# Reordering the attention stage of a retention + Mish + GLU kernel: weights decoded one round ahead, state copies first on ScalarE, v loaded before q and k

## The chip, the cores and the metric

The kernel runs on one core of a Trainium2 chip. The metric is the device time of one execution in microseconds. The engines are TensorE (PE in the profile, with its weight loads as PEld), VectorE (DVE), ScalarE (ACT), GpSimd (POOL) and SyncE (SP), which here issues nearly all transfers. Each engine works through its own queue in the order of issue.

## The reference

Three stages follow one another; the output of each is the input of the next. All data are float32.

```python
# 1: retention (linear attention with decay), B=2, H=8, S=768, D=64
for t in range(S):
    state = gamma * state + einsum('bhd,bhe->bhde', k[:, :, t], v[:, :, t])
    y[:, :, t] = D**-0.5 * einsum('bhd,bhde->bhe', q[:, :, t], state)
x = y.transpose(0, 2, 1, 3).reshape(1536, 512)
# 2: MLP, w_in 512 x 2048, w_out 2048 x 512
h = x @ w_in
x = (h * tanh(softplus(h))) @ w_out            # Mish
# 3: gated MLP, w_gate and w_val 512 x 1536, w_out 1536 x 512
out = (sigmoid(x @ w_gate) * (x @ w_val)) @ w_out
```

## The kernel before

The 1536 tokens are three chunks of 512 (`NCH`), or twelve blocks of 128 (`NSUB`); four blocks make a chunk (`SPC`), six blocks a batch entry (`SPB`).

**Two halves.** The first half, the attention stage, is issued exactly in the order of the code (`early` holds an element). After `early.clear()` the rest of the two MLPs is first recorded as nodes, and `replay()` issues them in an order that it plans from costs of its own; nothing in that second half is touched, and its plan starts from the same set of recorded nodes. At the seam, each engine goes on with the second half as soon as its queue has finished the first.

**Attention.** The products are small: a "quarter product" (`quarter`) is a 64x64 by 64x64 matmul that uses a quarter of the array. Block j needs `scores(j, r)` (k against q, masked by `mask` on VectorE into `a_t`), `state(j, s)` (k against the scaled v, `vp_t`, summed into one PSUM bank `st`), `keep` (ScalarE copies the running state out of that bank into `s_t`), and `outs(j, row)` (the block's own part and the part from the state). `at_prep(j)` is the GpSimd instruction that scales v into `vp`, and for j from 1 to 5 a second one that prepares a table `og`. `block(j)` issues, in this order: state and scores of block j+1 (first half) between the second row of outs of block j-1; the VectorE product that puts block j-1 into `acc_t`; `keep(j+1, 0)`; the first row of outs of block j between scores and state of block j+1 (second half); `mask`; `keep(j+1, 1)`. The second half's state products add to the bank that `keep(j+1, 0)` copies, so they wait for that copy, and the next block's state products wait for `keep(j+1, 1)`.

**Dense work inside the attention stage.** From block 4 on, one step of the first MLP is issued in each round. There are eight: `plain1(0)`, `plain1(1)` for the first chunk and `plain1(0, 1)`, `plain1(1, 1)` for the second, two steps each. A step is twelve 128x128 by 128x512 matmuls (`plain_steps`): values are split into a high and a low part, and each of four 128-row parts takes three products (high-high, high-low, low-high). Then ScalarE applies Mish (`e`), and `split` makes the high part on ScalarE and the low part on GpSimd (`g`). The split input of the first chunk is `xc` (`put_plain`), that of the second is `B11` and `B21` (`put_block`). The second chunk uses the weights of the first again.

**Weights.** They come as 512 KB pieces of 8-byte words (`load_piece`, two staging buffers `raw`) and are decoded by `decode`: two ScalarE instructions (`raw`, `v`), then two VectorE ones. `put` leaves the split (ScalarE `late_hi`, then VectorE or GpSimd `late_lo`) for later; `flush` issues what was left, `flush_hi` only the ScalarE part. `pump` flushes and then decodes one piece; `weight(key)`, which the dense step calls, flushes again.

**The round before** (`blocks`): `pump` (decode of the piece that this very round's dense step needs, in rounds 4 to 7), `block(j)` with `flush_hi()` in its middle, `at_prep(j+2)`, the loads, `load_piece`, in rounds 4 and 8 the split of the chunk's input, then the dense step, whose Mish and split stand last in ScalarE's queue. In rounds 8 to 11 the decoded piece belongs to `w_out` and no dense step of the stage needs it.

**Transfers.** k and v come together (`nv`, 3 buffers), q and k feature-major as `qk` (5 buffers), 512 KB each. Before, `load(jq, jn)` issues qk of block j+4 and then nv of block j+3, after block j.

Of the kernel before, what the change touches and what calls it, by code (L numbers as in the profile page):

```python
# [9 lines left out]
F32 = mybir.dt.float32  # L10
# [8 lines left out]
P = 128  # L19
# [4 lines left out]
def kernel(ctx, tc, qk, nv, w1i, w1o, w2g, w2v, w2o, ma_in, og_in, sg_in, ck_in, out):  # L24
# [12 lines left out]
    NSUB = qk.shape[0]  # L37
    KK = DM // P
    NP = KK
    D = P // 2  # L40
    FF1 = w1i.shape[0]
    FF2 = w2g.shape[0]
    N = 512
    NCH = NT // N
    SPC = N // P
    SPB = NSUB // 2
# [4 lines left out]
    AHEAD = 4  # L51
    Q = P // 2

    early = [True]
# [108 lines left out]
    dve = Queue(nc.vector, lambda n, kw: (0.157 + 0.00104 * n) * (1 if psum(kw) else 1.3), 0.1)  # L163
    act = Queue(nc.scalar, lambda n, kw: 0.17 + 0.0009 * min(n, N), 0.1)
    pool = Queue(nc.gpsimd, lambda n, kw: 0.08 + 0.00258 * n, 0.1)
    sync = Queue(nc.sync, lambda n, kw: 3.3 if isinstance(kw["out"], Part) else 1.6, 0.3)
# [98 lines left out]
    xc_t = big.tile([P, KK, 2, N], F32R, name="xc")  # L265
    acc_t = [big.tile([P, KK, N], F32, name=f"acc{c}") for c in range(NCH)]
    y_t = {"B11": xc_t[:, :2, :, :H], "B21": xc_t[:, 2:, :, :H], "T4": xc_t[:, :2, :, H:], "B22": xc_t[:, 2:, :, H:]}

    def split(raw, hi, lo, eng):
        act.activation(out=hi, in_=raw, func=AF.Copy)  # L270
        eng.tensor_tensor(out=lo, in0=raw, in1=hi.bitcast(F32), op=ALU.subtract)
# [33 lines left out]
    for f in range(FF2):  # L305
# [3 lines left out]
        a, q, w, o = [[(k, (2, f))] for k in "aqs"] + [[("o", (2, f - 1)), ("o", (2, f))] if f % 2 else []]  # L309
# [2 lines left out]
    raws, w_t, left = [], {}, {}  # L312
    owner = {r: [] for r in RINGS}
    cnt = {"dma": 0, "raw": 0, "task": 0}
    steps, late_hi, late_lo, sums_t, vs = [], [], [], {}, {}
    lo_eng = {"w": dve, "g": pool, "x": dve}

    def load_piece():
        n = cnt["dma"]
        if n >= len(pieces) or n >= cnt["raw"] + STG:  # L320
            return
        kind, i = pieces[n]
        t = stg.tile([P, DM], I64, tag="raw", name="raw")
        sync.dma_start(out=t, in_=src[kind][i])
        raws.append(t)
        cnt["dma"] += 1
# [40 lines left out]
    def put(key, v):  # L367
        t = slot(key)
        if home(key) == "q":
            v = v[:, H:]  # L370
        hi, lo = t[:, 0], t[:, 1]
        late_hi.append(lambda: act.activation(out=hi, in_=v, func=AF.Copy))
        late_lo.append(lambda: lo_eng["w"].tensor_tensor(out=lo, in0=v, in1=hi.bitcast(F32), op=ALU.subtract))
        if not early:
            flush()
# [36 lines left out]
    def flush_hi():  # L412
        while late_hi:
            late_hi.pop(0)()

    def flush():
        flush_hi()
        while late_lo:
            late_lo.pop(0)()

    def pump(n=1):
        flush()
        for _ in range(n):
            if not steps and not plan():
                return
            ring = steps[0][0]
            if not room(ring) if ring else "dcs" not in lo_eng:
                return
            steps.pop(0)[1]()

    def weight(key):
        while key not in w_t:
            if not steps:
                assert plan(), key
            steps.pop(0)[1]()
        flush()
        return w_t[key]

    def spend(key):
# [3 lines left out]

    def put_plain():
        for kk in range(KK):
            split(acc_t[0][:, kk], xc_t[:, kk, 0], xc_t[:, kk, 1], pool if early and kk > 1 else lo_eng["x"])

    def put_block(n, c, k0):
        for k in range(2):
            split(acc_t[c][:, k0 + k], b_t[n][:, k, 0], b_t[n][:, k, 1], pool if early and k0 else lo_eng["x"])  # L450
# [29 lines left out]
        return sums_of(acc_t[0][:, :, :H], acc_t[0][:, :, H:], y_t, H, pool if early else either)  # L480


    g_t = {}
    hx = {}

    def hbank():
# [105 lines left out]

    def put_g(e, key):
        g = gp.tile([P, 2, N], F32R, tag="g", name="g")
        split(e, g[:, 0], g[:, 1], lo_eng["g"])
        g_t[key] = g

    def mish(h, key):
        e = ep.tile([P, N], F32, tag="e", name="e")
# [81 lines left out]
    def run(*parts):  # L681
        for p in parts:
            for s in p:
                s()
# [22 lines left out]
    with ExitStack() as actx:  # L707
        ac = actx.enter_context(tc.tile_pool(name="ac", bufs=1))
        ldq = actx.enter_context(tc.tile_pool(name="ldq", bufs=AHEAD + 1))
        ldn = actx.enter_context(tc.tile_pool(name="ldn", bufs=AHEAD - 1))  # L710
# [8 lines left out]
        og_t = [ac.tile([P, NP, P], F32, name=f"og{b}") for b in range(SPB)]  # L719
        qk_t, nv_t, a_t, vp_t, st_t, s_t, sc_t, o_t = {}, {}, {}, {}, {}, {}, {}, {}  # L720

        def load(jq, jn):
            if jq < NSUB:
                qk_t[jq] = ldq.tile([P, 2, NP, P], F32, tag="qk", name="qk_t")
                sync.dma_start(out=qk_t[jq], in_=qk[jq])
            if jn < NSUB:
                nv_t[jn] = ldn.tile([P, 2, 2 * NP, D], F32, tag="nv", name="nv_t")
                sync.dma_start(out=nv_t[jn], in_=nv[jn])

        def at_prep(j):  # L730
            if j >= NSUB:
                return
            vp_t[j] = at3.tile([P, 2 * NP, D], F32, tag="vp", name="vp")
            pool.tensor_tensor(
                out=vp_t[j], in0=nv_t[j][:, 1], in1=ck[:, j % SPB].to_broadcast([P, 2 * NP, D]), op=ALU.mult
            )
            b = j % SPB
            if 0 < b == j:
                pool.tensor_tensor(out=og_t[b], in0=og_t[0], in1=sg[:, b].to_broadcast([P, NP, P]), op=ALU.mult)

        def rows(n):
            return slice(Q * n, Q * n + Q)

        def quarter(o, w, x, start=True, stop=True):
            pe.matmul(out=o, lhsT=w, rhs=x, start=start, stop=stop, skip_group_check=True)
# [15 lines left out]
        def mask(j):  # L761
            if j >= NSUB:
                return
            a_t[j] = a = at.tile([P, 2, NP, Q], F32, tag="a", name="a")
            for r in range(2):
                h = slice(r, NP - r, 3 - 2 * r)
                dve.tensor_tensor(out=a[:, :, h], in0=sc_t.pop((j, r))[:, :, h, :],
                                  in1=ma.to_broadcast([P, 2, NP // 2, Q]), op=ALU.mult)

        def state(j, s):  # L770

            if j >= NSUB:
                return [lambda: [quarter(st_t[0][rows(c), 0, :], z[rows(0), rows(0)], z[rows(0), rows(0)]) for c in range(2)]]
            v, k = vp_t[j], nv_t[j]
            new = j % SPB == 0 and s == 0
            if new:
                st_t[0] = ps_s.tile([P, NP, D], F32, tag="s", name="st")
            st = st_t[0]

            def pair(p):  # L780
                for e in range(2):
                    quarter(st[rows((e + p) % 2), p, :], k[rows(s), 0, 2 * p + e, :], v[rows(s), 2 * p + e, :],
                            new and p == 0, p == NP - 1)

            return [lambda p=p: pair(p) for p in range(NP)]

        def keep(j, s):
            s_t[2 * j + s + 1] = at6.tile([P, NP, D], F32, tag="s", name="s")
            act.activation(out=s_t[2 * j + s + 1], in_=st_t[0], func=AF.Copy)
# [25 lines left out]
                    if n < len(side):  # L815
                        side[n]()

        def block(j):

            lanes(state(j + 1, 0) + scores(j + 1, 0), outs(j - 1, 1))  # L820
            if j:
                b = (j - 1) // SPC, (j - 1) % SPC * P
                dve.tensor_tensor(out=acc_t[b[0]][:, :, b[1]:b[1] + P], in0=o_t[j - 1], in1=og_t[(j - 1) % SPB], op=ALU.mult)
            if j == NSUB:
                return
            keep(j + 1, 0)
            flush_hi()
            if j < NSUB - 1:
                lanes(outs(j, 0), scores(j + 1, 1) + state(j + 1, 1))
                mask(j + 1)  # L830
            else:
                run(outs(j, 0), state(j + 1, 1))
            keep(j + 1, 1)

        def blocks(j0, dense, made):

            for j in range(j0, j0 + SPC):
                lo_eng["w"] = pool if j >= SPB else dve
                if j >= SPC:
                    pump()  # L840
                block(j)
                at_prep(j + 2)
                load(j + AHEAD, j + AHEAD - 1)
                load_piece()
                if j == j0:
                    flush()
                    made()
                if dense:
                    dense.pop(0)()

        for t, table in ((ck, ck_in), (ma, ma_in), (og_t[0], og_in), (sg, sg_in)):
            act.dma_start(out=t, in_=table)
# [2 lines left out]
        z = ac.tile([P, NP * D], F32, name="z")  # L855
        dve.memset(ap=z, constant=0.0)
        for n in range(WARM):
            o = ps_o.tile([P, NP * D], F32, tag="o", name="warm")
            pe.matmul(out=o, lhsT=z[:, 0:P], rhs=z)
        for j in range(AHEAD):  # L860
            load(j, j if j < AHEAD - 1 else NSUB)
        at_prep(0)
        at_prep(1)
        lanes(scores(0, 0), scores(0, 1))
        mask(0)
        run(state(0, 0))
        keep(0, 0)
        run(state(0, 1))
        keep(0, 1)
        blocks(0, [], lambda: None)  # L870
        dense = plain1(0) + plain1(1) + plain1(0, 1) + plain1(1, 1)
        blocks(SPC, dense, put_plain)
        blocks(2 * SPC, dense, lambda: (put_block("B11", 1, 0), put_block("B21", 1, 2)))
        block(NSUB)
        run(dense)
        flush()

    early.clear()
# [105 lines left out]
```

## Time and profile before

| | us |
|---|---|
| median of three runs | 625.25 |
| lowest and highest | 622.3 and 625.29 |
| profiled execution, its own time | 624.73 |
| its span on the core | 622.8 |
| PE busy | 581.9 (93%) |
| POOL, DVE, ACT busy | 406.9, 371.3, 300.9 |
| mean granted TensorE clock | 0.972 of full |

The span runs from the first to the last instruction recorded on the core; the execution's own time is a little longer. A granted clock of 1.00 is 2.4 GHz, of 0.50 it is 1.2 GHz. A busy PE is not a PE at its peak: matmuls are pipelined, and in the attention stage many small ones overlap.

### The profile page before, as it was taken

What the parts mean: (1) busy time and instruction counts of PE and PEld (TensorE: products, weight loads), DVE (VectorE), ACT (ScalarE), POOL (GpSimd) and SP (SyncE); (2) the same over time, 40 slices, a digit from 0 to 9 for tenths busy, and PEclk for the clock granted to TensorE, in tenths of its full rate; (3) what the DMA queues carried; (4) which work ended last, traced back from release to release, by engine and by line L of the source; (5) the groups of instructions that cost most, each with busy time, mean ns of one, the idle gap of its engine ahead of it and who ended that gap; (6) DMA issues with size and microseconds to landing.
All of it is one profiled execution on the core that took longest, in us unless ns stands there. A gap on an engine that the chain in (4) does not pass through costs nothing.

```text
span 622.8 us, 10405 instructions
## 1 busy us (share of the span) xinstructions
PE 581.9 (93%) x4154; PEld 486.3 (78%) x4154; DVE 371.3 (60%) x530; ACT 300.9 (48%) x549; POOL 406.9 (65%) x349
## 2 busy tenths in 40 slices
PE   7567689999999999999999999999999999999997
PEld 6545467787788888888877867888888888888886
DVE  1352443414687968574787366689767766754554
ACT  1243346654766565533665546766544444440220
POOL 3343455999999686634799999897746745750220
PEclk7898789999999999999999999999999999999999
DMA  8763312300232324030322001333203114000004
GB/s 340 258 202 111 143 57 70 101 1 34 68 119 85 107 96 136 2 101 2 103 70 99 0 1 67 103 102 118 86 34 125 46 34 135 2 0 2 0 25 178
DMA packets 15599, 52.37 MB, mean 84 GB/s; under 512 B 2112, under 2 KB 2112, under 8 KB 15552
## 3 DMA queue, kind: packets, MB, share of 16 engines
q1 hardware_dynamic: 14976, 51.39, 24.2%
q8 instruction: 32, 0.52, 0.3%
q10 hardware_dynamic: 576, 0.33, 0.2%
q14 instruction: 15, 0.12, 0.1%
HBM read 48.57 MB, written 3.15 MB: 83 GB/s over the span
## 4 chain that ended last, share of the span: by engine, by line
PE 69%; POOL 16%; DVE 5%; ACT 5%; DMA 2%; issue 2%; SPq 0%; DVEq 0%; ACTq 0%; POOLq 0%
PE o L144 27%; PE h L144 26%; PE hx L144 14%; POOL t L144 5%; POOL T L144 4%; DMA nv_t<-nv 2%; DVE v L144 2%; DVE raw L144 1%; POOL g L144 1%; POOL B L144 1%; POOL YT L144 1%; POOL s L144 1%; PE st L144 1%; POOL ww L144 1%; POOL xc L144 1%
## 5 line engine op out<-in xcount | busy, mean ns | idle before, releaser
L144 POOL TENSOR_TENSOR g<-e,g 128x512 fp32r<-128x512 f32 x81 | 111.9, 1391 | 89.6 <-ACT g L144 85.2
L144 PE MATMUL o<-g,wo 128*128 128x512 f32 x576 | 140.1, 393 | 2.5 <-ACT acc L144 0.9
L144 DVE TENSOR_TENSOR acc<-o,acc 128x512 f32<-128x512 f32 x132 | 90.5, 688 | 66.4 <-PE o L144 65.5
L144 PEld LDWEIGHTS o<-g,wo 128*128 128x128 f32 x576 | 105.4, 188 | 25.8 <-DVE acc L144 2.7
L144 PE MATMUL o<-wo,g 128*128 128x512 f32 x432 | 108.9, 392 | 0.5 <-ACT acc L144 0.5
L144 DVE SCALAR_TENSOR_TENSOR raw<-raw 128x512 int32<-128x512 int32 x68 | 71.6, 1054 | 57.7 <-ACT raw L144 57.1
L144 PE MATMUL h<-B,ww 128*128 128x512 f32 x372 | 94.7, 391 | 0.0
L144 PE MATMUL h<-T,ww 128*128 128x512 f32 x360 | 91.4, 390 | 0.8 <-DVE u L144 0.8
L144 PEld LDWEIGHTS o<-wo,g 128*128 128x128 f32 x432 | 78.1, 189 | 15.4 <-ACT acc L144 1.3
L144 POOL TENSOR_TENSOR ww<-s,ww 128x512 fp32r<-128x512 f32 x35 | 50.4, 1444 | 53.7 <-ACT ww L144 53.7
L144 PEld LDWEIGHTS h<-B,ww 128*128 128x128 f32 x372 | 68.8, 188 | 14.1 <-DVE B L144 0.3
L144 PEld LDWEIGHTS h<-T,ww 128*128 128x128 f32 x360 | 67.2, 188 | 15.2 <-DVE u L144 1.2
L144 DVE SCALAR_TENSOR_TENSOR v<-v,raw 128x512 int32<-128x512 int32 x68 | 68.8, 1013 | 7.7 <-ACT v L144 4.9
L144 ACT ACTIVATE e<-h 128x512 f32<-128x512 f32 x57 | 33.8, 593 | 73.6 <-PE h L144 50.6
L144 ACT ACTIVATE raw<-raw 128x512 int32<-128x512 uint8 x68 | 45.4, 669 | 37.4 <-DMA raw<-w2g 14.1
L144 PE MATMUL hx<-xc,ww 128*128 128x256 f32 (+1 forms) x336 | 56.6, 306 | 5.1 <-ACT ww L144 2.0
L144 ACT ACTIVATE g<-e 128x512 fp32r<-128x512 f32 x84 | 51.7, 630 | 17.3 <-DVE e L144 16.2
L144 PEld LDWEIGHTS hx<-xc,ww 128*128 128x128 f32 x336 | 49.6, 194 | 11.8 <-ACT ww L144 2.1
L144 ACT ACTIVATE v<-raw 128x512 f32<-128x512 f32 x68 | 44.8, 663 | 16.2 <-POOL s L144 12.9
L144 DVE TENSOR_TENSOR h<-h,u 128x512 f32<-128x512 f32 x54 | 37.6, 695 | 21.4 <-PE h L144 21.1
L144 PEld LDWEIGHTS hx<-YT,ww 128*128 128x128 f32 x288 | 40.7, 190 | 6.8 <-DVE u L144 3.2
L144 PE MATMUL hx<-YT,ww 128*128 128x256 f32 x288 | 42.2, 283 | 2.4 <-DVE u L144 2.4
(79 smaller groups left out, 776.3 us busy)
## 6 DMA issues: line engine op xcount, KB each, us to landing
raw<-w1i SPq DMA_DIRECT2D x16, 512.0 KB, 3.4
raw<-w1o SPq DMA_DIRECT2D x16, 512.0 KB, 3.3
qk_t<-qk SPq DMA_DIRECT2D x12, 512.0 KB, 4.3
nv_t<-nv SPq DMA_DIRECT2D x12, 512.0 KB, 5.3
raw<-w2g SPq DMA_DIRECT2D x12, 512.0 KB, 3.2
raw<-w2v SPq DMA_DIRECT2D x12, 512.0 KB, 3.2
raw<-w2o SPq DMA_DIRECT2D x12, 512.0 KB, 3.3
out<-acc SPq DMA_DIRECT2D x12, 256.0 KB, 2.0
```

The lines of the kernel that those rows point to most:

```text
L144: i = call(**kw)
```

## The change

- Blocks 0 to 12 are one loop. `flush()` moves to the top of a round, ahead of `block(j)`; the decode (`feed`: `pump` and `load_piece`) moves from ahead of the block to behind it, and the dense step that uses the piece moves one round later: rounds 5 to 12 instead of 4 to 11. `weight` and `pump` no longer flush in this stage, except where the key is in `fresh`, that is, not yet flushed.
- On ScalarE, `keep` of a block now comes before the weight copies of the decode and before the split of the previous dense step's result, which `put_g` puts off into `late_g` and `block` issues behind `keep(j+1, 0)`. The same place takes `at_prep(j+2)` and, in rounds 5 and 9, one half of the input's split (`middle`); the other half is issued at the end of rounds 4 and 8.
- `load(j)` issues nv of a block and then its qk, both for block j+4 after block j. Three blocks are loaded ahead at the start instead of four qk and three nv.
- `warm(n)` issues 2n quarter products on zeros into a bank that nobody reads: 8 and 4 ahead of and between the first states, and 4 in each of rounds 0 to 3.

```diff
@@ put
+        fresh.add(key)
         late_hi.append(lambda: act.activation(out=hi, in_=v, func=AF.Copy))
@@ flush
         while late_lo:
             late_lo.pop(0)()
+        fresh.clear()
     def pump(n=1):
-        flush()
+        if not early:
+            flush()
@@ weight
-        flush()
+        if not early or key in fresh:
+            flush()
@@ put_g
-        split(e, g[:, 0], g[:, 1], lo_eng["g"])
         g_t[key] = g
+        late_g.append(lambda: split(e, g[:, 0], g[:, 1], lo_eng["g"]))
+        if not early:
+            late_g.pop(0)()
@@ load
-        def load(jq, jn):
-            if jq < NSUB:
-                qk_t[jq] = ldq.tile([P, 2, NP, P], F32, tag="qk", name="qk_t")
-                sync.dma_start(out=qk_t[jq], in_=qk[jq])
-            if jn < NSUB:
-                nv_t[jn] = ldn.tile([P, 2, 2 * NP, D], F32, tag="nv", name="nv_t")
-                sync.dma_start(out=nv_t[jn], in_=nv[jn])
+        def load(j):
+            if j < NSUB:
+                nv_t[j] = ldn.tile([P, 2, 2 * NP, D], F32, tag="nv", name="nv_t")
+                sync.dma_start(out=nv_t[j], in_=nv[j])
+                qk_t[j] = ldq.tile([P, 2, NP, P], F32, tag="qk", name="qk_t")
+                sync.dma_start(out=qk_t[j], in_=qk[j])
@@ block
-        def block(j):
+        def block(j, middle=lambda: None):
...
             keep(j + 1, 0)
-            flush_hi()
+            at_prep(j + 2)
+            middle()
+            while late_g:
+                late_g.pop(0)()
@@ blocks
-            for j in range(j0, j0 + SPC):
-                lo_eng["w"] = pool if j >= SPB else dve
-                if j >= SPC:
-                    pump()
-                block(j)
-                at_prep(j + 2)
-                load(j + AHEAD, j + AHEAD - 1)
-                load_piece()
-                if j == j0:
-                    flush()
-                    made()
-                if dense:
-                    dense.pop(0)()
@@ the stage
+        def warm(n):
+            x = hx["pool"].tile([P, N], F32, tag="x0", name="hx")
+            for m in range(n):
+                for c in range(2):
+                    quarter(x[rows(c), rows(0)], z[rows(0), rows(0)], z[rows(0), rows(0)])
+
-        for j in range(AHEAD):
-            load(j, j if j < AHEAD - 1 else NSUB)
+        for j in range(AHEAD - 1):
+            load(j)
         at_prep(0)
         at_prep(1)
         lanes(scores(0, 0), scores(0, 1))
         mask(0)
+        warm(8)
         run(state(0, 0))
         keep(0, 0)
+        warm(4)
         run(state(0, 1))
         keep(0, 1)
-        blocks(0, [], lambda: None)
+        load(AHEAD - 1)
         dense = plain1(0) + plain1(1) + plain1(0, 1) + plain1(1, 1)
-        blocks(SPC, dense, put_plain)
-        blocks(2 * SPC, dense, lambda: (put_block("B11", 1, 0), put_block("B21", 1, 2)))
-        block(NSUB)
-        run(dense)
+        def feed():
+            pump()
+            load_piece()
+
+        def plain(k0):
+            for kk in (k0, k0 + 1):
+                split(acc_t[0][:, kk], xc_t[:, kk, 0], xc_t[:, kk, 1], pool if kk > 1 else dve)
+
+        for j in range(NSUB + 1):
+            lo_eng["w"] = pool if j >= SPB else dve
+            flush()
+            if j == SPC + 1:
+                block(j, lambda: plain(2))
+            elif j == 2 * SPC + 1:
+                block(j, lambda: put_block("B21", 1, 2))
+            else:
+                block(j)
+            if j < SPC:
+                warm(4)
+            load(j + AHEAD)
+            if j in (1, SPC - 1):
+                load_piece()
+            if SPC <= j < NSUB:
+                feed()
+            if j == SPC:
+                plain(0)
+            elif j == 2 * SPC:
+                put_block("B11", 1, 0)
+            if j > SPC:
+                dense.pop(0)()
+            while j >= NSUB and late_g:
+                late_g.pop(0)()
         flush()
```

## Rows read from the trace of the kernel before

**Rows 1.** The page: the span, and the granted clock in 40 equal slices.

```profile
span 622.8 us, 10405 instructions
...
PEclk7898789999999999999999999999999999999999
```

**Rows 2.** Windows: stretch, busy of PE, PEld, DVE, ACT, POOL, then clock, DMA share, GB/s.

```profile
40.00:50.00 10.00, 6.52 (x106) 4.53 (x105) 4.50 (x6) 2.80 (x7) 2.52 (x2) 0.83 0.51 157
...
90.00:100.00 10.00, 7.94 (x215) 6.67 (x213) 4.87 (x7) 6.12 (x12) 4.09 (x4) 1.00 0.23 86
...
120.00:130.00 10.00, 10.00 (x45) 8.26 (x44) 2.04 (x2) 8.20 (x16) 9.92 (x10) 1.00 0.09 33
```

**Rows 3.** The chain in order of time, one round: start, us, what.

```profile
44.98 4.17 PE h L144 x10
49.18 0.61 ACT e L144
49.80 0.63 ACT g L144
50.44 0.57 ACT raw L144
51.03 1.32 DVE raw L144
52.45 1.35 DVE v L144
53.82 0.64 ACT ww L144
54.52 1.28 POOL ww L144
55.85 4.14 PE hx L144 x10
```

**Rows 4.** The chain, the last dense steps and the seam.

```profile
93.39 2.96 PE hx L144 x12
...
99.47 2.96 PE h L144 x12
...
103.85 1.30 POOL g L144
105.14 0.70 POOL t L144
```

**Rows 5.** PE's timeline, the starts of blocks 0 and 2.

```profile
10.48 1.12 PE L144 MATMUL st<-vp,nv_t 64*64 64x64 f32 x16 [0.97 <-POOL vp L144]
...
19.02 0.27 PE L144 MATMUL st<-vp,nv_t 64*64 64x64 f32 x2 [0.54 <-issue]
```

**Rows 6.** The chain around block 4 and the first dense step.

```profile
20.65 7.42 DMA nv_t<-nv
...
29.88 0.37 PE st L144 x2
...
38.46 0.61 ACT e L144
```

**Rows 7.** PE's waits from 0 to 105 us: us in total, times, longest.

```profile
PE ao L144 <- issue: 4.4, 2, 3.3
```

**Rows 8.** Windows: a stretch with quarter products alone, columns as in rows 2.

```profile
10.00:12.00 2.00, 1.52 (x28) 1.52 (x30) 0.00 (x0) 0.34 (x1) 1.48 (x3) 0.50 1.04 416
```

**Rows 9.** POOL's timeline: scaling of v; two low parts of the input.

```profile
51.75 1.49 POOL L144 TENSOR_TENSOR vp<-nv_t,ck 128x512 f32<-128x512 f32 x1
...
78.61 2.96 POOL L144 TENSOR_TENSOR B<-acc,B 128x512 fp32r<-128x512 f32 x2 [0.56 <-ACT B L144]
```

**Rows 10.** ACT's timeline: one state copy; four input copies in a row.

```profile
51.45 0.36 ACT L144 ACTIVATE s<-st 128x256 f32<-128x256 f32 x1
...
76.87 2.18 ACT L144 ACTIVATE B<-acc 128x512 fp32r<-128x512 f32 x4
```

**Rows 11.** DVE's timeline: a decode while POOL is idle.

```profile
30.37 0.69 DVE L144 SCALAR_TENSOR_TENSOR raw<-raw 128x512 int32<-128x512 int32 x1 [1.36 <-ACT raw L144]
```

More of the change, by code (lines that the diff above doesn't have):

```diff
@@ L314 @@
     cnt = {"dma": 0, "raw": 0, "task": 0}
-    steps, late_hi, late_lo, sums_t, vs = [], [], [], {}, {}
+    steps, late_hi, late_lo, fresh, sums_t, vs = [], [], [], set(), {}, {}
     lo_eng = {"w": dve, "g": pool, "x": dve}
@@ L445, in put_plain @@
         for kk in range(KK):
-            split(acc_t[0][:, kk], xc_t[:, kk, 0], xc_t[:, kk, 1], pool if early and kk > 1 else lo_eng["x"])
+            split(acc_t[0][:, kk], xc_t[:, kk, 0], xc_t[:, kk, 1], lo_eng["x"])
     def put_block(n, c, k0):
@@ L480, in side_sums @@
         return sums_of(acc_t[0][:, :, :H], acc_t[0][:, :, H:], y_t, H, pool if early else either)
-    g_t = {}
+    g_t, late_g = {}, []
     hx = {}
@@ L833, in block @@
             keep(j + 1, 1)
-        def blocks(j0, dense, made):
-            for j in range(j0, j0 + SPC):
-                lo_eng["w"] = pool if j >= SPB else dve
-                if j >= SPC:
-                    pump()
-                block(j)
-                at_prep(j + 2)
-                load(j + AHEAD, j + AHEAD - 1)
-                load_piece()
-                if j == j0:
-                    flush()
-                    made()
-                if dense:
-                    dense.pop(0)()
         for t, table in ((ck, ck_in), (ma, ma_in), (og_t[0], og_in), (sg, sg_in)):
@@ L865 @@
         mask(0)
+        warm(8)
         run(state(0, 0))
         keep(0, 0)
+        warm(4)
         run(state(0, 1))
         keep(0, 1)
-        blocks(0, [], lambda: None)
+        load(AHEAD - 1)
         dense = plain1(0) + plain1(1) + plain1(0, 1) + plain1(1, 1)
-        blocks(SPC, dense, put_plain)
-        blocks(2 * SPC, dense, lambda: (put_block("B11", 1, 0), put_block("B21", 1, 2)))
-        block(NSUB)
-        run(dense)
+        def feed():
[28 more added lines that the diff above has]
+                late_g.pop(0)()
+        assert not dense
         flush()
```

## Prediction

> **What bounds the kernel now.** I read the page first [rows 1]: the granted clock falls below full in the first quarter of the span and nowhere behind it. The windows say why that quarter is worth looking at [rows 2]: between 40 and 50 us TensorE is busy 6.52 us of 10 and no other engine more than 4.5, so nothing is full and something is waiting in turn; between 90 and 100 us it is 7.94; between 120 and 130 us TensorE is busy 10.00 and GpSimd 9.92. What is saved ahead of about 105 us is therefore saved out of waiting, and behind it there is no idle time in which a saving could vanish.
>
> The chain of waits shows the turn itself [rows 3]. One round from 44.98 to 55.85, 10.87 us, is a single file through four engines: ten of the twelve dense matmuls 4.17, Mish .61, high part of its result .63, decode on ScalarE .57, decode on VectorE 1.32 and 1.35, high and low part of the new weights .64 and 1.28, and then the next dense step. These eight sum to 10.57, so a hand-over costs about .04. The block's attention products are nowhere in the file: they run beside it. The last rounds need no new weights; there twelve matmuls take 2.96 and a round 99.47 - 93.39 = 6.08 [rows 4]. The last dense step ends at 99.47 + 2.96 = 102.43, GpSimd finishes that step's low part and starts the second half at 105.14 (2.71 later) [rows 4], and from there its queue is nearly gapless.
>
> Ahead of the rounds, blocks 0 and 1 take 19.02 - 10.48 = 8.54, 4.27 each [rows 5]. Block 4 starts at 29.88, behind a v whose transfer was issued at 20.65 and took 7.42; the first dense step ends where its Mish starts, at 38.46 [rows 6]. So blocks 2 and 3 took 10.86, of which TensorE spent 4.4 in two waits for nothing that the trace names [rows 7].
>
> **The change part by part.** I measure everything up to the moment when GpSimd starts the second half, since that queue is the one without gaps. The second half itself is the same list of work.
>
> *Start to block 4.* v comes before q and k, but the first scores need q and k, which are now second in the queue, and the first states need v: one wait shrinks and the other grows, so I price the first block's start (10.48) at no change; it could move by one 512 KB transfer, about 1.3 us at the 416 GB/s of the row [rows 8]. The v of block j+4 is issued at the end of block j and needed at the start of block j+3. Its issue waits for its buffer, which the second half of block j frees, and q and k are queued behind it on SP; they are needed no sooner, so that costs nothing as long as the transfer and its scaling fit into two blocks. Do they? The block without the unnamed waits is (10.86 - 4.4)/2 = 3.2, and 7.42 + 1.49 for the scaling [rows 6, 9] is 8.9, more than two such blocks. So v still ends last: for block 4 it is issued at the end of block 1, 19.0, and block 4 starts at 19.0 + 8.9 = 27.9. Lower bound 19.0 + 2 x 3.2 = 25.5, if transfers are quicker with fewer queued. Upper bound: both unnamed waits stay, 29.9, and the added zero products show. Eight of them are about what the sixteen records of the state products are, 1.12 at the low clock [rows 5]; they stand where TensorE waits for a state copy of .36 [rows 10], so up to .75 a round shows, 3.0 in four rounds: 32.9. I take 27.9, gain 2.0.
>
> On the unnamed waits the Trainium skill ("Runtime: NRT & Kernel Launch", section "Instruction fetch mechanics") says that engines stream their instructions by a queue of their own and that crossing from one block of them to the next is mostly hidden. By that they would not recur, and block 4 would start when v allows, 27.9, as I have it; by the trace, which shows 4.4 us of waits it cannot name, 29.9 and a time 2.0 longer. No row shows that they are fetches.
>
> *Block 4 to the end of the first dense step.* Before, 38.46 - 29.88 = 8.58. After, the dense step waits for a round more, but its input's split is what ends last: block 4 3.2; two decode instructions on ScalarE 1.14 (both priced as the first, .57); two input copies 1.09 (half of 2.18 [rows 10]); the weights' high part .64; the state copy .36; the third input copy .55; the two low parts on GpSimd 2.96 [rows 9]; the last three matmuls .74. Sum 10.7: a loss of 2.1.
>
> *The rounds.* Seven intervals lie between the first and the last dense step, 102.43 - 38.46 = 63.97 before, 9.1 each. After, the decode of round j is for the dense step of round j+1, so the file breaks into shorter ones, and the longest sets the round:
> - Weights: dense 2.96, Mish .61, high part .64 (ScalarE now has them in this order), low part 1.28, dense: 5.49, with four hand-overs 5.65.
> - Decode against state copies: the high part stands ahead of the state copies on ScalarE and waits for VectorE. High part .64, copy .36, state products .6 (an estimate, half of the 1.12 of [rows 5] at the full clock), copy .36, decode .57, 1.32, 1.35: 5.20, with hand-overs 5.5. The previous result's high part (.63) lies beside the state products.
> - TensorE: block 3.2 (with its two copy waits) and dense 2.96: 6.16.
>
> I take 6.0, between the files and the last. Lower bound 5.6; upper 6.8, if the weights' high part (.64), now ahead of the copies, shows in TensorE's 6.16. These take the dense step at 2.96, the full clock, which the last rounds have with much the same mixture [rows 2, 4].
>
> VectorE's decode instruction takes .69 with GpSimd idle [rows 11] and 1.32 in the file, where GpSimd works; I keep 1.32 since GpSimd has 1.28 + 1.49 + 1.28 of work in each round. The Trainium skill ("SBUF — State Buffer", section "Who interferes with whom") says that a VectorE instruction with two SBUF inputs and a GpSimd one that reads SBUF exclude each other, the second waiting until the first has finished. By that an instruction could wait for a whole low part, and the round would be the third rival's below.
>
> In round 9 the second chunk's halves come on GpSimd behind the weights' low part and the scaling of v: .61 + .64 + 1.28 + 1.49 + 2.96 = 6.98, hand-overs .2, the last three matmuls .74: 7.9 instead of 6.0, so 2.0 more. Seven intervals: 7 x 6.0 + 2.0 = 44.0, a gain of 20.0.
>
> *The seam.* Block 12 now precedes the last dense step, so the last state work is out of the way. But two put-off results remain: Mish .61, two high parts .63 each (the second beside the first low part), two low parts of 1.28: .61 + .63 + 2.56 and hand-overs .2 = 4.0 instead of 2.71, a loss of 1.3.
>
> *At no price:* flushing elsewhere and `fresh` (the weights of a dense step were flushed at the round's top; no key is fresh); the staging transfers, whose piece is needed two rounds, 12 us, later (7.42 was the longest flight I rest on); q and k behind v.
>
> Sum: 2.0 - 2.1 + 20.0 - 1.3 = 18.6. From the profiled execution's own 624.73 that is 606.1, and I predict 606.0. The median of the runs shown is .5 above that execution, within their own spread of 3 us.
>
> **The rivals.**
> *The clock stays low (the other sign).* A stretch with quarter products alone had .50 [rows 8], the dense matmuls of the round shown took .417 each, twelve of them 5.0, and the added zero products are such small ones. Then a round is block 4.27 and dense 5.0, 9.3; GpSimd's work in round 9 is hidden (0); seven intervals 65.1, a loss of 1.1; block 4 at 10.5 + 4 x 4.27 + 4.4 = 32.0, a loss of 2.1; with 2.1 and 1.3 in all 6.6: 631.3. It turns the sign where the round exceeds (63.97 - 2.0 + 2.0 - 2.1 - 1.3)/7 = 8.65. Against it: from 90 us on the clock is 1.00 although TensorE idles a fifth of the time [rows 2], and the low clock in the round shown follows some 6 us in which TensorE waited for the file, which is what goes.
> *The second half gives it back.* Its order is planned as if every engine were free at once, and a late low part at the seam could hold TensorE. If half is lost: 624.73 - 9.3 = 615.4. Against it: both TensorE and GpSimd are full there [rows 2], and 1.3 is already counted.
> *The decode does not get out of the way.* It still passes ScalarE behind two state copies, and VectorE beside GpSimd. If each of its two VectorE instructions waits out a low part, .69 + 1.28 = 1.97, the second file grows by 1.27 to 6.8 and with exposed copies to 7.0: seven times 1.0 more, 613.1. Against it: the two durations in the chain, 1.32 and 1.35, where GpSimd worked beside them [rows 3].
>
> **How the numbers follow.** The forecast has .73, the third rival .12, the second .06, the clock .05, and .04 is for what I have not seen, half of it no gain at all. The forecast's own bounds: 25.5 and 5.6 give 606.1 - 2.4 - 2.8 = 600.9; 32.9 and 6.8 give 606.1 + 5.0 + 5.6 = 616.7, but not both at once. The range, 599.5 to 614.5, takes in the third rival and a start earlier by one transfer. Half a per cent, 3.1 us, is about what a measurement can tell here: faster .93, same .03, slower .04.
>
> **What would show it.** Right: twelve dense matmuls at about 2.9 from round 6 on; ScalarE's decode beginning while TensorE is still in its block or dense step, not after Mish; about 6 us from one Mish to the next and 8 at the fifth; the last dense step ending near 27.9 + 10.7 + 44.0 = 82.6 and GpSimd beginning the second half near 86.6; the rest of the trace as before, shifted. Wrong: a clock of .5 in the rounds; a VectorE decode over 1.5; block 4 after 30 us; or a second half longer than 624.73 - 105.14 = 519.6 by more than 1.

## The result, and the profile after

The changed kernel takes 606.38 us (median of four runs, 604.67 to 607.81), the kernel before on the same chip 625.27 (622.3 to 627.85): a ratio of 0.970, 95% interval 0.965 to 0.975. The profiled execution took 605.99, its span 604.2. The forecast was 606.0.

First the page after, against [rows 1]: the span and the clock, which falls below 0.9 in three of the 40 slices instead of five; its mean is 0.988 instead of 0.972.

```profile
span 604.2 us, 10628 instructions
...
PEclk9879998999999999999999999999999999999999
```

Now the chain of waits of the changed kernel in order of time (start, us, what), from the first long wait to the seam, against [rows 3, 4, 6].

```profile
11.95 1.49 issue
...
15.76 3.15 issue
...
22.64 1.19 issue
...
26.57 3.21 issue
...
31.64 0.23 PE st L144 x2
...
36.53 3.27 issue
...
47.38 2.98 PE h L144 x12
...
52.66 3.00 PE hx L144 x12
...
57.95 2.97 PE h L144 x12
...
64.92 2.93 POOL B L144 x2
...
82.86 0.60 ACT e L144
...
84.05 2.54 POOL g L144 x2
86.59 0.69 POOL t L144
```

Read it from below. GpSimd starts the second half at 86.59 instead of 105.14. The last Mish starts at 82.86. The dense steps at 47.38, 52.66 and 57.95 stand 5.3 apart, at the full clock, and in between the chain holds only TensorE: the single file of [rows 3] is gone. One step waits for GpSimd's two low parts of the second chunk (64.92). But ahead of block 4, which starts at 31.64, the chain holds two waits of over 3 us and two of over 1 us that it calls "issue", which is time in which the engine waited for nothing that the trace shows; a third of over 3 us (36.53) falls into the work behind it.

ScalarE's timeline shows the first Mish, at which the first dense step has ended (against the last row of [rows 6]), and a round in the order that was built: Mish, the weights' high part, the state copy, the previous result's high part, the second state copy, the decode.

```profile
45.26 0.60 ACT L144 ACTIVATE e<-hx 128x512 f32<-128x512 f32 x1 [2.30 <-PE hx L144]
...
50.40 0.60 ACT L144 ACTIVATE e<-h 128x512 f32<-128x512 f32 x1 [1.46 <-PE h L144]
51.03 0.63 ACT L144 ACTIVATE ww<-v 128x512 fp32r<-128x512 f32 x1
51.56 0.37 ACT L144 ACTIVATE s<-st 128x256 f32<-128x256 f32 x1
51.83 0.62 ACT L144 ACTIVATE g<-e 128x512 fp32r<-128x512 f32 x1
52.72 0.39 ACT L144 ACTIVATE s<-st 128x256 f32<-128x256 f32 x1 [0.27 <-PE st L144]
53.00 0.66 ACT L144 ACTIVATE raw<-raw 128x512 int32<-128x512 uint8 x1
53.56 0.65 ACT L144 ACTIVATE v<-raw 128x512 f32<-128x512 f32 x1
```

ScalarE's part of the decode ends at 54.21, inside the dense step (52.66 to 55.66); VectorE's part follows until 56.28 (its rows stand further below). ScalarE now waits for TensorE and no longer the other way round. The windows say the same of TensorE, busy all of 50 to 60 us (columns as in [rows 2]):

```profile
50.00:60.00 10.00, 10.00 (x271) 8.04 (x270) 7.10 (x11) 7.52 (x16) 7.42 (x7) 1.00 0.83 271
```

TensorE's waits from 0 to 90 us (total, times, longest), against [rows 7], name the new cost:

```profile
PE ao L144 <- issue: 7.7, 3, 3.3
PE hx L144 <- issue: 4.6, 2, 3.1
...
PE st L144 <- issue: 1.4, 3, 0.6
```

13.7 us without a named cause. In the kernel before, the first form of wait came to 4.4, the second did not occur, and the third came to .5. The third form is another thing: its waits end about .1 after ScalarE's copy of the state has ended (a copy from 9.26 to 9.64, then products at 9.74), so 12.3 us are left without a cause. Terms against the forecast:

| term | forecast | measured |
|---|---|---|
| start to block 4 | 27.9 | 31.64 |
| block 4 to the first dense end | 10.7 | 45.26 - 31.64 = 13.6 |
| seven intervals of dense steps | 44.0 | 82.86 - 45.26 = 37.6 |
| last dense end to GpSimd's start of the second half | 4.0 | 86.59 - 82.86 = 3.7 |
| GpSimd's start of the second half | 86.6 | 86.59 |
| from there to the end of the execution | 519.6 | 605.99 - 86.59 = 519.4 |

The number came out to the tenth because three terms were wrong by +3.7, +2.9 and -6.4 and nearly cancelled: that it fits so well is luck. The experiments ask what carried the gain, and what the unnamed waits are.

### The profile page after: what moved, and what is told of

Its sections match the earlier page's. It is cut to its first block, busy times and chain, and to the rows that moved or that the text cites. A ratio compares the mean times of both kernels' runs of the same rounds, so it can differ in the third digit from the quotient of the medians.

```text
span 604.2 us, 10628 instructions
## 1 busy us (share of the span) xinstructions
PE 575.4 (95%) x4266; PEld 483.8 (80%) x4266; DVE 371.3 (61%) x529; ACT 300.7 (50%) x549; POOL 407.4 (67%) x350
## 3 DMA queue, kind: packets, MB, share of 16 engines
HBM read 48.57 MB, written 3.15 MB: 86 GB/s over the span
## 4 chain that ended last, share of the span: by engine, by line
PE 77%; POOL 12%; DVE 4%; issue 4%; ACT 1%; DMA 1%; SPq 0%; DVEq 0%; POOLq 0%; ACTq 0%
PE o L144 29%; PE h L144 27%; PE hx L144 16%; POOL t L144 4%; POOL T L144 3%; PE ao L144 2%; PE st L144 2%; POOL g L144 2%; DVE v L144 1%; POOL YT L144 1%; POOL s L144 1%; PE sc L144 1%; POOL B L144 1%; DVE raw L144 1%; DMA qk_t<-qk 1%
## 5 line engine op out<-in xcount | busy, mean ns | idle before, releaser
L144 POOL TENSOR_TENSOR g<-e,g 128x512 fp32r<-128x512 f32 x81 | 113.5, 1413 | 64.2 <-ACT g L144 59.8
L144 DVE SCALAR_TENSOR_TENSOR raw<-raw 128x512 int32<-128x512 int32 x68 | 68.2, 1003 | 31.8 <-ACT raw L144 31.4
L144 DVE SCALAR_TENSOR_TENSOR v<-v,raw 128x512 int32<-128x512 int32 x68 | 73.9, 1088 | 7.9 <-ACT v L144 6.5
L144 PE MATMUL hx<-xc,ww 128*128 128x256 f32 (+1 forms) x336 | 54.9, 302 | 0.9 <-DVE hx L144 0.9
L144 POOL TENSOR_TENSOR ww<-v,ww 128x512 fp32r<-128x512 f32 x23 | 32.7, 1423 | 17.7 <-ACT ww L144 17.7
```

The source lines that it names most:

```text
L144: i = call(**kw)
```

## The experiments

Theory: the decode a round ahead carries the gain, with the state copies first on ScalarE adding to it; TensorE's own instructions, not v, are late in the first blocks. Each run changes the changed kernel; times are medians beside runs of the kernel before, with the ratio to it and its interval.

**Without the products on zeros** (e1).

```diff
-        warm(8)
-        warm(4)
-            if j < SPC:
-                warm(4)
```

> The changed kernel without its products on zeros. Theory (instruction supply): TensorE's unnamed waits recur after about every 255 of its instructions, so 224 records fewer (112 products, 112 weight loads) save nearly one wait of about 3.2 us; block 4 starts near 28.5 us instead of 31.6 and the time is about 603.5. Rival (clock): the zero products hold the clock at full from 4 to 18 us and without them it is 0.50 there; each of blocks 0 to 2 takes about 1 us longer, block 4 starts at 33 or later, time 607 or more.

601.43 us, 0.963 (0.958 to 0.967): 5.0 faster than with them. The first Mish starts at 40.53 instead of 45.26, and block 4 at 27.6, .9 ahead of the 28.5 expected. The clock does fall, as its windows show, where the changed kernel has 1.00 and 0.84:

```profile
16.00:18.00 2.00, 1.46 (x53) 1.30 (x49) 0.42 (x1) 0.38 (x1) 0.00 (x0) 0.50 0.19 68
18.00:20.00 2.00, 2.00 (x87) 2.00 (x83) 0.37 (x1) 0.38 (x1) 1.15 (x2) 0.50 0.90 315
```

So the zero products do hold the clock, and yet are a loss. The gain is larger than the 3 us expected, and the rival's 607 is out.

**The loads of the kernel before** (e2): q and k first, then v, four and three ahead.

```diff
-            load(j + AHEAD)
+            load(j + AHEAD, j + AHEAD - 1)
```

> The changed kernel with the loads of the kernel before (q and k of block j+4, then k and v of block j+3, after block j; four and three at the start). Theory (instruction supply): v is not what comes last in blocks 0 to 4, so block 4 starts within 1 us of 31.6 and the time is 605.5 to 607.5. Rival (the prediction's own term): v's flight and scaling set the start of block 4, and half a block less of lead costs about 2 us: block 4 at 33.5, time 608.5.

606.92 us, 0.971 (0.967 to 0.974), against 606.38: no difference that these runs can tell. Block 4 starts at 31.57 against 31.64, although the state products of block 1 began 1.25 later (10.99 against 9.74). The order of transfers gave nothing, and the prediction's term for v, worth 2 us, is not supported.

**The result's split at once** (e3).

```diff
-        late_g.append(lambda: split(e, g[:, 0], g[:, 1], lo_eng["g"]))
-        if not early:
-            late_g.pop(0)()
+        split(e, g[:, 0], g[:, 1], lo_eng["g"])
```

> The changed kernel with the dense result's split issued at once, so that ScalarE makes its high part right behind Mish, ahead of the weights' high part and the state copies. Theory (TensorE sets the round, 5.2 us, and a state copy that comes 0.63 later shows): the second half of a block waits, rounds of 5.5 to 5.8, seven of them, time 609 to 610. Rival (hidden): the copy has more than 0.63 to spare in the block, rounds stay at 5.2 to 5.3 and the time at 606 to 607, or lower by the 1.3 us that one low part at the seam costs.

612.27 us, 0.979 (0.974 to 0.984): 5.9 slower, more than expected, and for another reason. The four runs scatter, from 609.53 to 614.71. The chain of waits of the profiled one (614.23), one round:

```profile
46.72 0.61 ACT e L144
47.35 0.64 ACT g L144
48.06 0.53 POOL g L144
48.59 0.70 issue
49.29 1.30 POOL ww L144
50.63 2.57 PE h L144 x10
53.23 0.61 ACT e L144
```

The round is 53.23 - 46.72 = 6.5. What ends last is not a state copy, as I had written, but GpSimd's work: the result's low part (g, 48.06 to 49.34) stands ahead of the weights' low part (ww), for which the next dense step waits. A state copy is late too, and TensorE waits .48 for one in this round, but the low part comes later still. The high part on ScalarE, .64 ahead of GpSimd's g, lies on the same path. So in these rounds putting the split off is worth most as an order for GpSimd. In the same execution the round with the second chunk's low parts took 9.5 instead of 7.4, and the next 7.1 instead of 5.2, with a granted clock of 0.50 from 74 to 80 us.

**The decode and its dense step in one round again** (e4).

```diff
             flush()
+            if SPC <= j < NSUB:
+                pump()
             block(j)
...
             if SPC <= j < NSUB:
-                feed()
+                load_piece()
...
-            if j > SPC:
+            if SPC <= j < NSUB:
                 dense.pop(0)()
```

> The changed kernel with the decode ahead of the block and the dense step in the same round again, all else kept (state copies first, put-off split, loads, zero products). Theory (the decode one round ahead carries the gain): the single file of Mish, decode, split is back, rounds of 9 to 10.5 us for the first four and 6 for the others, time 622 to 627. Rival (state copies first carries it): rounds of 6.5 to 7, time 611 to 615.

621.34 us, 0.995 (0.992 to 0.998). The four first Mish start at 43.01, 53.34, 63.97 and 72.22, so rounds of 10.3, 10.6 and 8.3, then 9.6 and later ones of 6.3: the file is back. TensorE waits again, and the granted clock falls with it (0.57 from 50 to 54 us, 0.63 from 78 to 82), so a part of the price is clock. The edit also puts both halves of the input's split back to the end of rounds 4 and 8, because the dense step of the same round needs them; what that costs by itself was not measured. The time, .7 below the expected range, is far from the rival's 611 to 615.

**Neither** (e10): the edits of e3 and e4 together.

> The changed kernel with both the decode in the same round and the split at once; loads and products on zeros stay. Theory (decode ahead and state copies first are the gain, the rest costs): rounds of 10 to 11 us and then 6 to 6.5, as before, and the products on zeros on top, 626 to 629. Rival (the two parts don't add): 620 to 623, as with the decode alone undone.

629.64 us, 1.006 (1.004 to 1.008), .6 above the expected range; the later rounds took 6.9, where 6 to 6.5 was expected. The rest of the change (loads, products on zeros, the places of `flush` and `at_prep`) is by itself slightly slower than the kernel before. With this the four kernels make a square: the decode ahead is worth 621.34 - 606.38 = 15.0 with the split put off and 629.64 - 612.27 = 17.4 without; the split put off is worth 5.9 and 8.3. The four did not all run side by side; by their ratios to the kernel before, the decode ahead is worth 2.5 and 2.7 hundredths and the split put off 0.9 and 1.1. The parts nearly add.

**Half of the transfers** (e5), a single execution: q and k are loaded for the first three blocks and used again, so the attention of the later ones is computed from the wrong q and k.

```diff
-                qk_t[j] = ldq.tile([P, 2, NP, P], F32, tag="qk", name="qk_t")
-                sync.dma_start(out=qk_t[j], in_=qk[j])
+                if j < AHEAD - 1:
+                    qk_t[j] = ldq.tile([P, 2, NP, P], F32, tag="qk", name="qk_t")
+                    sync.dma_start(out=qk_t[j], in_=qk[j])
+                else:
+                    qk_t[j] = qk_t[j % (AHEAD - 1)]
```

> The changed kernel with q and k loaded for the first three blocks only, and used again for the others, so that the attention of blocks 3 to 11 is computed from the wrong q and k; half of the stage's transfers fall away, all instructions of TensorE stay. Theory (TensorE's instructions come through the same transfer engines and stand behind the data): the unnamed waits keep their places in the instruction count, but shrink from 3.2 us to about 1.2, as the one that fell into a stretch without transfers; 14 us in all become 6 to 8 and block 4 starts near 25. Rival (the supply is slow by itself): the waits stay at 3 us and block 4 near 31.

601.21 us. TensorE's waits of the kind fall to 9.8 us (4.8, 3.6 and 1.4), the longest to 2.7:

```profile
PE ao L144 <- issue: 4.8, 3, 2.7
PE hx L144 <- issue: 3.6, 2, 2.3
```

Between the two: the state copy ahead of block 4 starts at 28.76 instead of 31.02. The transfers lengthen the waits, by about 4 us of 13.7, but most of the time stays, with half of the transfers still running. The waits keep their places in the count of records, of which more below. The 6 to 8 that I had expected is missed.

**Wide products on zeros** (e6): a ninth of the records (24 instead of 224). TensorE's time for them was meant to be the same; in the chain it is 2.5 us instead of 3.7.

```diff
-            for m in range(n):
-                for c in range(2):
-                    quarter(x[rows(c), rows(0)], z[rows(0), rows(0)], z[rows(0), rows(0)])
+            pe.matmul(out=x[:, 0:32 * n], lhsT=z[:, 0:P], rhs=z[:, 0:32 * n], start=True, stop=True, skip_group_check=True)
```

> The changed kernel with each group of products on zeros replaced by one 128-row product of about the same TensorE time (8 small ones, 16 records of about 0.47 us in all, by one 128-column product, two records of about 0.4 us). Theory (instruction supply): the records are what cost, block 4 starts about 3 to 4 us earlier than with the small ones and the time is near 602. Rival (the zero products cost their own time on TensorE, some 3 us of the 5 that leaving them out gave): block 4 stays within 1.5 us of 31.6 and the time is 605 or more.

603.29 us, 0.965 (0.959 to 0.970), between the theory's 602 and the rival's 605. The first Mish starts at 39.57, 5.7 earlier, and block 4 at 26.3, 5.3 earlier (27.7 in e9 below, with the same instructions up to there): more than all the time on zeros that the chain of the changed kernel holds. So most of what the small ones cost was not their time on TensorE. A later round took some of it back: the fifth interval between Mish starts is 6.5 where e1 has 5.2, with a granted clock of 0.50 from 64 to 66 us. Now the decisive view. I let windows end inside the long waits and read how many matmuls and weight loads TensorE had done by then (the counts behind PE and PEld). The changed kernel:

```profile
0.00:12.40 12.40, 10.07 (x222) 8.30 (x223) 1.94 (x6) 3.02 (x6) 5.01 (x9) 1.00 0.86 321
0.00:17.00 17.00, 12.40 (x350) 10.49 (x350) 3.29 (x9) 3.79 (x8) 7.37 (x11) 1.00 0.89 333
0.00:23.20 23.20, 16.13 (x477) 14.05 (x478) 4.64 (x12) 4.17 (x9) 9.41 (x13) 0.93 0.83 310
0.00:28.00 28.00, 18.64 (x604) 16.31 (x605) 6.00 (x15) 4.94 (x11) 11.46 (x15) 0.94 0.77 288
0.00:38.00 38.00, 24.79 (x859) 22.11 (x859) 9.62 (x21) 8.49 (x19) 13.71 (x17) 0.91 0.72 259
```

The kernel with wide zeros:

```profile
0.00:14.76 14.76, 10.97 (x222) 8.65 (x222) 2.63 (x7) 3.40 (x7) 6.70 (x11) 1.00 0.88 337
0.00:18.69 18.69, 13.76 (x349) 11.11 (x350) 3.48 (x9) 4.17 (x9) 8.55 (x13) 1.00 0.86 327
0.00:24.30 24.30, 16.50 (x477) 13.48 (x477) 4.83 (x12) 4.93 (x11) 11.46 (x15) 1.00 0.87 322
0.00:28.66 28.66, 20.15 (x604) 16.66 (x604) 6.19 (x15) 5.70 (x13) 12.50 (x16) 0.95 0.83 306
```

And the kernel before, in its two waits of [rows 7]:

```profile
0.00:20.80 20.80, 15.21 (x348) 13.33 (x349) 3.88 (x10) 4.17 (x9) 7.36 (x11) 0.75 0.87 325
0.00:26.00 26.00, 17.57 (x475) 15.40 (x475) 5.86 (x14) 4.93 (x11) 9.40 (x13) 0.80 0.86 319
```

Add the two counts of a row: 445, 700, 955, 1209 and 1718 after; 444, 699, 954 and 1208 with wide zeros; 697 and 950 before. The waits stand 253 to 255 records apart, or twice that, whatever work lies there and whenever that is. From 1209 to 1718 there are two stretches, and the boundary between them passed without a long wait. Two of the waits shown in the chain end at 15.76 + 3.15 = 18.91 and 26.57 + 3.21 = 29.78, two stretches apart, so a stretch of 255 takes 5.4 us, waits included. The small products on zeros are 112 matmuls and 112 weight loads; 224/255 of 5.4 is 4.8, and leaving them out gave 5.0. The Trainium skill ("Runtime: NRT & Kernel Launch", "Instruction fetch mechanics") says that instructions are refilled in blocks of 256; the spacing in the rows agrees with that number to within three. It also says that crossing a block is mostly hidden; here it is not, with waits of 1.2 to 3.3 us at five of six boundaries in the changed kernel. The trace has the packets too, of 16 KB, in the queue that it calls instruction. In the changed kernel they start at 10.9, 16.4, 21.6, 27.1 and 36.8 us, and the five waits end at 13.44, 18.91, 23.83, 29.78 and 39.79. In the first 46 us of the twelve traces 46 waits of over .35 us stand at such counts; they last .4 to 3.9 us, and each ends 1.2 to 1.6 us after the end of such a packet.

**The seam, two versions** (e7, e8). Both leave the products on zeros out and issue the seventh result's split ahead of the last dense step; e8 also gives the last two low parts to VectorE (the diff's first two lines).

```diff
+            if j == NSUB:
+                lo_eng["g"] = dve
+            while j >= NSUB and late_g:
+                late_g.pop(0)()
             if j > SPC:
                 dense.pop(0)()
             while j >= NSUB and late_g:
                 late_g.pop(0)()
```

> No products on zeros, and in round 12 the split of the seventh dense result is issued ahead of the last dense step instead of behind it. Theory (at the seam GpSimd's queue sets the end): its first work of the second half starts 1.3 us earlier against the last Mish, and the time is 1.3 lower than without the zero products alone, 600.2. Rival (TensorE sets the end there): no change from 601.4.

> As the one before, and the last two low parts at the seam go to VectorE, which is idle there for 9 us. Theory (GpSimd's queue sets the end): it starts the second half up to 3.8 us earlier against the last dense step, TensorE's wait of 3.3 us near 88 us goes, and the time is 597.5 to 598.5. Rival (TensorE or the second half's order sets the end): 600 to 601.5.

602.65 us, 0.963 (0.957 to 0.968), for e7: by its time no change. In its trace the step from the last Mish (80.21) to GpSimd's start of the second half (82.79) is 2.6 instead of 3.7 in e1, as expected; its first dense step came .8 later than e1's, and its rounds took 1.3 more, at a granted clock of 0.56 and 0.59 from 64 to 68 us, where e1 has 1.00; together that hides it. 599.47 us, 0.958 (0.952 to 0.964), for e8, 1.0 above the expected range. GpSimd in e1, then in e8, at the seam:

```profile
79.33 2.54 POOL L144 TENSOR_TENSOR g<-e,g 128x512 fp32r<-128x512 f32 x2 [2.75 <-ACT g L144]
81.83 0.74 POOL L144 TENSOR_TENSOR t<-acc 128x256 f32<-128x256 f32 x1
```

```profile
76.40 1.30 POOL L144 TENSOR_TENSOR wo<-v,wo 128x512 fp32r<-128x512 f32 x1 [2.39 <-ACT wo L144]
77.65 1.19 POOL L144 TENSOR_TENSOR t<-acc 128x256 f32<-128x256 f32 x1
```

In e8 the second half starts on GpSimd before the last Mish (79.25). And TensorE at the same place, its wait in e1 and in e8:

```profile
86.78 5.52 PE L144 MATMUL o<-g,wo 128*128 128x512 f32 x17 [3.30 <-ACT acc L144]
```

```profile
84.85 5.74 PE L144 MATMUL o<-g,wo 128*128 128x512 f32 x24 [0.26 <-ACT acc L144]
```

From the last Mish to the end of the span e1 takes 599.2 - 78.14 = 521.1, e7 520.0, e8 518.2: GpSimd's queue does set the end there, and 2.9 us were to be had. The medians show 2.0 of it, since e8's first dense step came 1.1 later than e1's (41.67).

**Wide zeros and the seam** (e9): the edits of e6 and e8, without leaving products out.

> The wide products on zeros instead of the small ones, and the last two low parts at the seam on VectorE, issued early. Theory (few records and a full clock): the first dense step ends 1 to 2 us before that of the kernel without products on zeros, near 39.5 to 40.5, and the time is 597 to 599. Rival (the clock ahead of the rounds is worth nothing): the first dense step ends at 41 to 42 and the time is 599 to 601.

599.95 us, 0.958 (0.956 to 0.960), no better than e8. Its first Mish starts at 42.66, outside both expectations, where e6, with the same instructions up to there, had 39.57. So the first stage scatters by 3 us from run to run, and the five kernels without small zero products (39.57 to 42.66) cannot be ranked among themselves; the three with them, with the decode ahead and all transfers (45.26 in the changed kernel, 46.25 in e2, 46.72 in e3) lie clear of them.

## Why the prediction was right, and where its steps were not

- **The single file breaks up: right.** e4 and the square show that the decode a round ahead carries 15.0 to 17.4 us; the clock stayed full in the rounds from 50 us on, and the first rival with its 8.65 us a round is out. One reading in that rival was off: in the 6.7 us of the file TensorE did not wait for some 6, it was busy for 3.0 of them, mostly with the block's products.
- **The rounds, 6.0: too long by .9.** 4.9 to 5.3 was measured, 7.7 for the one with the second chunk's low parts (forecast 7.9), 4.0 for the last, which has only the rest of a block. The mis-sized term is TensorE's block, 3.2. It was taken from blocks 2 and 3 of the kernel before, in which TensorE also stood .86 and .60 ahead of state products, for GpSimd's scaled v and a state copy; in the rounds these are hidden, and a block is 52.66 - 50.36 = 2.3. Block and dense step, 2.3 + 3.0, are the round. My file through the weights, 5.65, came out shorter too: a dense step needs the weights' low part only in its third matmul.
- **Start to block 4, 27.9: the failed step.** I let v's flight set it and took the unnamed waits as hidden behind it. e2 shows that v's lead did not matter; the counts show that TensorE's instruction stream did. I had its trace, [rows 7], and set it aside. The start at 10.48, priced at no change, came at 9.74, so from there to block 4 the miss is larger, 4.5. Of the 3.0 that the zero products might cost at most, as TensorE time, e1 found 5.0, most of it as records. A wait of 3.27 also fell into block 5, and the first dense step took 3.9 instead of 3.0, at a granted clock of 0.50 to 0.68 from 40 to 44 us; these two are more than the first dense step's 2.9, since part of them lies beside GpSimd's work on the input.
- **The unnamed waits, cause.** That they are bound to the place in the instruction stream is shown by the counts. That each ends a fixed time after a packet of instructions has come is shown by the 46 ends, however long the wait; so late instructions are the cause, as far as a trace can show it. What fills the 1.2 to 1.6 us between packet and end, and why the packets come no sooner, is not shown. That transfers lengthen the waits is shown in part, by one execution (e5).
- **Two of the prediction's own signs of being wrong came:** block 4 after 30 us (31.64), and a VectorE decode of over 1.5 (1.60). The total hid both.
- **The third rival, VectorE behind GpSimd.** It holds in kind: beside GpSimd's scaling of v and a low part, which itself took 1.76 instead of 1.3, one of the two decode instructions took .88 and the other 1.60 (VectorE's timeline), together 2.48 against 1.32 + 1.35. The Trainium skill's rule ("SBUF — State Buffer", "Who interferes with whom"), that one waits for the other to finish, fits a long and a short one better than two of 1.3. It did not lengthen the round, because the file with it, 5.3, is no longer than TensorE's; but nothing is to spare, since the decode ends at 56.28 and the weights' high part starts at 56.31.

```profile
53.70 0.88 DVE L144 SCALAR_TENSOR_TENSOR raw<-raw 128x512 int32<-128x512 int32 x1 [1.05 <-ACT raw L144]
54.68 1.60 DVE L144 SCALAR_TENSOR_TENSOR v<-v,raw 128x512 int32<-128x512 int32 x1
```

- **The second half gives nothing back: right,** 519.4 against 519.6. The seam cost 3.7 (4.0 forecast) and need not: e8.

## What to carry to other kernels

When a chain of waits runs through four engines in turn and none is full, look for the instruction that stands behind another's result only by its place in a queue; issuing it one round ahead took 15 us out here. A wait that the trace calls "issue" should be priced, not set aside: count the instructions between such waits and look for the packets that bring them, and if the count is constant, save records, not engine time. And a total that comes out right says little about its terms; compare each with the trace.

## What was not expected of the hardware

In the stage of small products TensorE waited 1.2 to 3.3 us after about every 255 matmul and weight-load records, 5.4 us a stretch with the wait, and each wait ended 1.2 to 1.6 us after the end of a 16 KB packet of instructions. In the two rounds from 47.38 to 57.95 it did about 545 records in 10.6 us, 5.0 us for 255, without such a wait: there the work itself takes nearly as long.

A full clock was worth less than it seemed: without small products on zeros the clock was 0.50 from 16 to 20 us, and the first dense step still ended 4.7 us earlier. And the clock is not the same in every execution: behind the same two waits of TensorE for the second chunk's low parts it fell to between 0.50 and 0.59 in e6 and e7 and stayed at 1.00 in the changed kernel and e1, which is 1.0 to 1.3 us of that round. Why it fell in some is not shown.
